# A linear-attention and two-stage expert kernel: two products moved from GpSimd to VectorE, a scan one unit later, one block's transposes sooner

## The chip, the core and the metric

One core of one Trainium2 chip runs the whole program. The metric is the device time of one execution in microseconds (us), the median of several runs. PE is TensorE, PEld its weight loads, DVE is VectorE, ACT is ScalarE, POOL is GpSimd, SP is the queue of SyncE, which issues nearly all loads.

## What is computed

Three layers follow each other. The first is a recurrent attention over 768 steps for 4 batches and 8 heads of width 48; its output is 3072 tokens of 384 numbers. The second is a gated layer without experts, and the third routes each token to two of eight experts.

```python
for t in range(S):                               # attention, per batch and head
    cur = np.einsum('bhd,bhe->bhde', u[None] * kt, vt)
    y[:, :, t] = np.einsum('bhd,bhde->bhe', rt, state + cur)
    state = wt[:, :, :, None] * state + np.einsum('bhd,bhe->bhde', kt, vt)
...
h = (x @ w1) * (x @ w2) @ w3                     # second layer
x = h @ w_out
...
out[mask] += top2_w[mask, k, None] * (np.maximum(x[mask] @ w1[e], 0.0) @ w2[e])
```

## The kernel before, in words

The tokens are cut into 24 chunks of 128 (six chunks for each batch) and 12 groups of two chunks. For the second layer the kernel first multiplies w3 by w_out, so that afterwards one matrix with 384 columns, and 16 columns for the routing of the third layer beside them, takes the place of two. This first stage is the one that the change touches. Each matrix is held as a high and a low part, so a product takes three matmuls (mm3, lines 193 to 196: high by high on line 194, high by low on 195, low by high on 196).

The work of the first stage comes in units u. A unit takes block u of w_out (128 x 384, cv_wo, only for u below 8) and block u of w3 (128 x 512, cv_w3). For each block ACT converts the top bits (line 149, tile top), DVE joins them with the middle bits (line 160 in the units written out by hand, line 178 later, tile cvz), ACT or DVE rounds this to the high part (167 or 180; WBh for w_out, w3h for w3), and DVE subtracts to get the low part (171 or 185; WBl, w3l). The joined w_out block is also transposed on PE (wo_T, line 420), copied out of PSUM (copy_T, lines 427 and 429, tile woT), multiplied by the routing weights (gate_cols, line 434), and the resulting 16 columns are split into high and low parts (gate_split, lines 139 and 140). mm_w3(u) then multiplies the w3 block by the finished w_out block. Units 0 to 2 are written out by hand in first_units (lines 444 to 492), where PE, DVE and ACT keep the order of the program. The loop of lines 619 to 637 runs units 3 to 18: at its start it converts, and the conversion calls flush, which joins and subtracts what the call before left open.

DVE keeps the order of the program throughout. The other engines are ordered by a planner until they are also put into program order (PE from group 2, ACT in the last group).

Between the units lie the attention's steps. WHEN (lines 548 to 553) gives, for each of the first six chunks, the slot of each of fourteen steps, in the order of STEPS (line 391). A slot of u - 24 up to u - 23.5 runs in the first half of unit u, ahead of mm_w3 and gate_split; the half unit after that runs behind wo_T. The steps that matter here, with their place in a line of WHEN counted from 0:

- 5, pre_scan (line 220): one DVE instruction that runs the product of the decays along the chunk (tile fg). It needs the load dtc.
- 9, pre_rec(j, 0) (lines 234 and 235): Ln and Exp on ACT, which give the reciprocals of fg (tile rc).
- 6, pre_rec(j, 1) (238 and 239): two DVE instructions that refine them. 7, pre_k, and 8, pre_r (do_r): two DVE instructions each, which scale k and r. do_r also issues the load dtc of chunk j + 2.
- 10, do_u: pre_u (lines 255 and 256), two products of 128 x 384 on the tile rku: r by k, and that by u. It also issues load_rk(j + 2), the load of r and k (tile nrk, two buffers) on SP.
- 11, pre_c (line 262): DVE sums the products of each head to cc. 12, pre_d (line 268): ACT spreads them over the diagonals of the tile am. 3, do_ov (line 280): DVE copies the masked attention products into am.
- 2, at_A (275), 4, do_T (285 and 287), 0, do_kv (308, then 315, 316 and 320) and 1, do_y (344, then 350 and 351): the attention's matmuls and what follows them. The last one leaves the tokens in high and low parts (xh, xl).

Behind the first stage the groups run: mo_ab (w1 and w2), mo_x (the merged matrix), then the routing; behind them the experts.

Of the kernel before, what the change touches and what calls it, by code (L numbers as in the profile page):

```python
# [71 lines left out]
def tile_kernel(ctx: ExitStack, tc: tile.TileContext, dt, nat, w3t, wout, w1, w2, e1, e2, cf, ci, out):  # L72
    nc = tc.nc
    pe, act, dve, pool, sp = nc.tensor, nc.scalar, nc.vector, nc.gpsimd, nc.sync
# [6 lines left out]
    class Pinned:  # L81
        on = False
# [7 lines left out]
    def f(ap):  # L90
        return ap.bitcast(F32)
# [14 lines left out]
    def c(n):  # L106
        o, w = CF[n]
        return cft[:, o:o + w]
# [29 lines left out]
    def split(h, l, src, on=None):  # L138
        act.copy(out=h, in_=src)
        (on or dve).tensor_tensor(out=l, in0=src, in1=f(h), op=OP.subtract)  # L140
# [18 lines left out]
    def join(mid, t, z, h, l, post):  # L159
        dve.scalar_tensor_tensor(z, mid, 13, t, op0=OP.logical_shift_right, op1=OP.bitwise_or)  # L160
        x = z.bitcast(F32)
        if post:
            post(x)
        return h, l, x

    def high(h, l, x, on=None):
        (on or act.copy)(out=h, in_=x)
        return h, l, x

    def lower(h, l, x):  # L170
        dve.tensor_tensor(out=l, in0=x, in1=f(h), op=OP.subtract)
# [21 lines left out]
    def mm3(o, wh, wl, xh, xl, start, stop, pin=lambda x: x):  # L193
        pin(pe.matmul(o, wh, xh, start=start, stop=False))  # L194
        pe.matmul(o, wh, xl, start=False, stop=False)  # L195
        pe.matmul(o, wl, xh, start=False, stop=stop)  # L196
# [54 lines left out]

    def pre_u(j):
        t = att.tile([P, DM], F32, name="rku", bufs=1)
        on = dve if 2 <= j < 5 else pool
        on.tensor_tensor(out=t, in0=RK[j][:, :DM], in1=RK[j][:, DM:], op=OP.mult)  # L255
        on.tensor_tensor(out=t, in0=t, in1=c("u"), op=OP.mult)
        KS["u", j] = t
# [106 lines left out]
    def do_u(j):  # L364
        pre_u(j)
        if j + 2 < NCH:
            load_rk(j + 2)
# [46 lines left out]
    def cv_wo(j, queue=True):  # L414
        return cvt(rawx["o", j], DM, woh[:, j, :DM], wol[:, j, :DM], post=lambda x: xo_.__setitem__(j, x), queue=queue)

    def wo_T(j, then=None):
        bank = PB[4 + j % 2]
        for kb in range(3):
            pe.transpose(bank[:, P * kb:P * kb + P], xo_[j][:, kb * P:kb * P + P], ident)  # L420
        (then or (lambda: copy_T(j)))()

    def copy_T(j):
        bank = PB[4 + j % 2]
        xo_[j] = fold.tile([P, DM], F32, name="woT")
        if j < 6:
            dve.tensor_copy(out=xo_[j], in_=bank[:, :DM])
        else:
            act.copy(out=xo_[j], in_=bank[:, :DM])

    def gate_cols(j):
        g = bK[:, 256 + 32 * j:272 + 32 * j]
        for kb in range(3):
            pe.matmul(g, xo_[j][:, P * kb:P * kb + P], wgn[:, kb], start=kb == 0, stop=kb == 2)  # L434

    def gate_split(j):
        split(woh[:, j, DM:], wol[:, j, DM:], bK[:, 256 + 32 * j:272 + 32 * j])

    def cv_w3(u, o=0, n=512, queue=True):
        if not o:  # L440
            w3s[u] = [fold.tile([P, 512], F32R, name=x, bufs=3) for x in ("w3h", "w3l")]
        return cvt(rawx["3", u], n, *[t[:, o:o + n] for t in w3s[u]], o, queue=queue)

    def first_units():
        x = cv_wo(0, False)
        o = high(*join(*x), dve.tensor_copy)
        wo_T(0, lambda: None)
        x = cv_w3(0, 0, 256, False)
        a = high(*join(*x))
        copy_T(0)  # L450
        warm_up(1)
        gate_cols(0)
        lower(*o)
        lower(*a)
        gate_split(0)
        mm_w3(0, (0, 1))
        x = cv_wo(1, False)
        o = join(*x)
        wo_T(1, lambda: None)
        x = cv_w3(0, 256, 256, False)  # L460
        b = join(*x)
        high(*o)
        high(*b)
        copy_T(1)
        lower(*b)
        mm_w3(0, (2,))
        gate_cols(1)
        x = cv_w3(1, 0, 256, False)
        a = high(*join(*x))
        lower(*o)  # L470
        gate_split(1)
        mm_w3(0, (3,))
        lower(*a)
        mm_w3(1, (0, 1))
        x = cv_w3(1, 256, 256, False)
        b = join(*x)
        x = cv_wo(2, False)
        high(*b)
        o = join(*x)
        lower(*b)  # L480
        mm_w3(1, (2,))
        wo_T(2, lambda: None)
        copy_T(2)
        mm_w3(1, (3,))
        x = cv_w3(2, queue=False)
        a = join(*x)
        high(*o)
        high(*a)
        gate_cols(2)
        lower(*o)  # L490
        gate_split(2)
        lower(*a)

    def mm_w3(u, fbs=range(4)):
        jb = u % 8
        for fb in fbs:
            s = slice(fb * P, fb * P + P)
            mm3(PB[fb][:, :XW], w3s[u][0][:, s], w3s[u][1][:, s], woh[:, jb, :], wol[:, jb, :], jb == 0, jb == 7,
                tc.keep_in_program_order if u == 15 else lambda x: x)
            if u == 7:  # L500
                split(W0[0][:, fb], W0[1][:, fb], PB[fb][:, :XW])
# [38 lines left out]
    def at(slot, fn, *a):  # L540
        todo.setdefault(slot, []).append((fn, a))

    def run_todo(lo, hi):
        for slot in sorted(x for x in todo if lo <= x < hi):
            for fn, a in todo.pop(slot):
                fn(*a)

    WHEN = {0: (-12.5, -11.5, -13.5, -12.5, -15.0, -20.6, -18.0, -17.05, -17.0, -20.0, -19.0, -16.5, -12.6, 0),
# [26 lines left out]
    for i, fn in enumerate(STEPS):  # L575
        for j in range(NCH):
            late = 3 if j == NCH - 1 and i == 1 else 0
            at(WHEN[j][i] if j in WHEN else 6 * j - 14 + LATE[i] - late, fn, j)
    at(-3, flush)
# [21 lines left out]
    def warm_up(n):  # L601
        for _ in range(n):
            tc.keep_in_program_order(pe.matmul(PB[6], warm, warm[:, None, :].to_broadcast([P, 4, P]), start=True, stop=True))
# [12 lines left out]
    with tc.manual_schedule(engines={mybir.EngineType.DVE, mybir.EngineType.PE, mybir.EngineType.Activation}):  # L616
        first_units()
# [718 lines left out]
```

## Time and profile before

| | before |
|---|---|
| median of 3 runs | 887.4 us (887.29 to 888.32) |
| profiled execution, its own time | 885.38 us |
| span of the profiled execution, first to last instruction | 883.6 us |
| PE busy | 867.0 us (98%) |
| DVE busy | 498.1 us (56%) |
| ACT busy | 435.9 us (49%) |
| POOL busy | 242.6 us (27%) |

The page gives each engine's busy time over the whole span. A busy share of 56% says nothing of one stage, so the trace is also read by stretches, and where two engines are both nearly always busy it is read instruction by instruction: the start, the duration, and in brackets the idle time of the engine just before, with what ended it. The chain of work that ended last follows the end of the program back, at each step to what released it.

### The profile page before, as it was taken

What the parts mean: (1) busy time and instruction counts of PE and PEld (TensorE: products, weight loads), DVE (VectorE), ACT (ScalarE), POOL (GpSimd) and SP (SyncE); (2) the same over time, 40 slices, a digit from 0 to 9 for tenths busy, and PEclk for the clock granted to TensorE, in tenths of its full rate; (3) what the DMA queues carried; (4) which work ended last, traced back from release to release, by engine and by line L of the source; (5) the groups of instructions that cost most, each with busy time, mean ns of one, the idle gap of its engine ahead of it and who ended that gap; (6) DMA issues with size and microseconds to landing.
All of it is one profiled execution on the core that took longest, in us unless ns stands there. A gap on an engine that the chain in (4) does not pass through costs nothing.

```text
span 883.6 us, 18266 instructions
## 1 busy us (share of the span) xinstructions
PE 867.0 (98%) x7325; PEld 807.5 (91%) x7325; DVE 498.1 (56%) x1219; ACT 435.9 (49%) x880; POOL 242.6 (27%) x216
## 2 busy tenths in 40 slices
PE   8999999999999999999999999999999999999996
PEld 5789899999999999999999989899998998989896
DVE  6899874866756856765475453352534434343430
ACT  5777665566466456555454343433433344343431
POOL 2010021041141141232344443407052260603113
PEclk9999999999999999999999999999999999999999
DMA  9956399668476566443365798829467393854213
GB/s 344 387 212 210 93 129 238 163 142 220 119 200 162 156 180 127 96 122 108 83 164 121 187 246 210 211 56 240 85 182 185 94 212 67 245 118 102 27 14 47
DMA packets 124255, 139.22 MB, mean 158 GB/s; under 512 B 75008, under 2 KB 103680, under 8 KB 124160
## 3 DMA queue, kind: packets, MB, share of 16 engines
q1 hardware_dynamic: 100624, 109.58, 45.9%
q0 software_dynamic: 12160, 19.72, 11.8%
q10 hardware_dynamic: 11376, 8.65, 3.1%
q8 instruction: 59, 0.97, 0.5%
q14 instruction: 36, 0.29, 0.1%
HBM read 88.12 MB, written 36.04 MB: 141 GB/s over the span
## 4 chain that ended last, share of the span: by engine, by line
PE 89%; DVE 6%; ACT 2%; issue 1%; DMA 0%; POOL 0%; SPq 0%; POOLq 0%; DVEq 0%; ACTq 0%
PE pb L194 27%; PE pb L195 26%; PE pb L196 26%; PE pb L344 3%; PE pb L275 3%; PE pb L1014 1%; DVE cvz L178 1%; PE pb L308 1%; DVE fg L222 0%; DVE w3l L185 0%; DVE am L280 0%; DVE WAl L185 0%; DMA rawf<-w3t 0%; PE pb L434 0%; ACT top L149 0%
## 5 line engine op out<-in xcount | busy, mean ns | idle before, releaser
L1019 POOL DMA_INDIRECT out<-ye,ti x49 | 77.0, 1572 | 225.7 <-ACT ye L1009 205.3
L992 DVE SCALAR_TENSOR_TENSOR HH<-pb,HH 128x256 fp32r<-128x256 f32 (+1 forms) x128 | 71.2, 557 | 110.6 <-ACT HH L991 110.6
L194 PE MATMUL pb<-XTh,WAh 128*128 128x512 f32 (+1 forms) x384 | 131.7, 343 | 0.0
L196 PE MATMUL pb<-XTh,WAl 128*128 128x512 f32 (+1 forms) x384 | 131.4, 342 | 0.0
L195 PE MATMUL pb<-XTl,WAh 128*128 128x512 f32 (+1 forms) x384 | 131.0, 341 | 0.0
L194 PE MATMUL pb<-WBh,HH 128*128 128x384 f32 x384 | 129.3, 337 | 0.0
L196 PE MATMUL pb<-WBh,HH 128*128 128x384 f32 x384 | 128.4, 334 | 0.0
L195 PE MATMUL pb<-WBl,HH 128*128 128x384 f32 x384 | 128.3, 334 | 0.0
L991 ACT ACTIVATE HH<-pb 128x256 fp32r<-128x256 f32 (+1 forms) x128 | 62.8, 492 | 115.4 <-PE pb L196 113.3
L824 POOL DMA_INDIRECT slots<-g_sc,g_si x48 | 51.7, 1077 | 125.2 <-DVE g_si L823 69.5
L1009 ACT ACTIVATE ye<-pb,ti 128x384 f32<-128x384 f32 x42 | 24.4, 582 | 124.2 <-PE pb L196 124.2
L195 PE MATMUL pb<-xl,WAh 128*128 128x256 f32 x288 | 80.8, 281 | 0.8 <-DVE xl L351 0.8
L194 PE MATMUL pb<-xh,WAh 128*128 128x256 f32 x288 | 81.5, 283 | 0.0
L194 PE MATMUL pb<-xh,WBh 128*128 128x256 f32 x288 | 81.2, 282 | 0.0
L195 PE MATMUL pb<-xl,WBh 128*128 128x256 f32 x288 | 81.0, 281 | 0.0
L196 PE MATMUL pb<-xh,WBl 128*128 128x256 f32 x288 | 81.0, 281 | 0.0
L196 PE MATMUL pb<-xh,WAl 128*128 128x256 f32 x288 | 80.9, 281 | 0.0
L195 PEld LDWEIGHTS pb<-XTl,WAh 128*128 128x128 f32 x384 | 72.3, 188 | 7.6
L196 PEld LDWEIGHTS pb<-XTh,WAl 128*128 128x128 f32 x384 | 72.2, 188 | 7.6
L194 PEld LDWEIGHTS pb<-XTh,WAh 128*128 128x128 f32 x384 | 72.0, 188 | 7.5
L194 PEld LDWEIGHTS pb<-WBh,HH 128*128 128x128 f32 x384 | 72.1, 188 | 5.0 <-ACT WAh L892 4.4
L255 POOL TENSOR_TENSOR rku<-nrk 128x384 f32<-128x384 f32 x21 | 21.7, 1031 | 197.7 <-DVE cc L262 80.8
(208 smaller groups left out, 2065.7 us busy)
## 6 DMA issues: line engine op xcount, KB each, us to landing
dtc<-dt SPq DMA_DIRECT2D x24, 772.0 KB, 5.2
raw<-e SPq DMA_DIRECT2D x18, 768.0 KB, 5.5
raww<-e SPq DMA_DIRECT2D x14, 768.0 KB, 5.2
nrk<-nat SPq DMA_DIRECT2D x24, 384.0 KB, 6.8
expert_rows<-xg SPq DMA_DIRECT2D x45, 192.0 KB, 6.1
rawf<-w3t SPq DMA_DIRECT2D x14, 512.0 KB, 7.2
nv<-nat SPq DMA_DIRECT2D x24, 256.0 KB, 5.4
out<-zeros SPq DMA_DIRECT2D x9, 576.0 KB, 5.4
```

Source lines behind the costliest of these rows:

```text
L178: dve.scalar_tensor_tensor(z, mid, 13, t, op0=OP.logical_shift_right, op1=OP.bitwise_or)
L194: pin(pe.matmul(o, wh, xh, start=start, stop=False))
L195: pe.matmul(o, wh, xl, start=False, stop=False)
L196: pe.matmul(o, wl, xh, start=False, stop=stop)
L255: on.tensor_tensor(out=t, in0=RK[j][:, :DM], in1=RK[j][:, DM:], op=OP.mult)
L275: pe.matmul(bST[hb][:, P * a:P * a + P], KT[j][q, a].rearrange("p s i -> p (s i)"), RT[j][q, a].rearrange("p s i -> p (s i)"), start=True, ...
L344: pe.matmul(o, lt, rh, start=st, stop=en, tile_position=tp)
L824: ins = pool.indirect_dma_start(out=table, out_offset=bass.IndirectOffsetOnAxis(ap=si[:, i, k:k + 1], axis=0), in_=SC[:, i, k, :], in_offs ...
L991: act.activation(out=Hh[hf][:, ff], in_=bank[:, :n], func=AF.Relu)
L992: dve.scalar_tensor_tensor(Hl[hf][:, ff], bank[:, :n], 0.0, f(Hh[hf][:, ff]), op0=OP.max, op1=OP.subtract)
L1009: act.activation(out=y[:n], in_=bank[:n], func=AF.Copy, scale=wt)
L1019: ins = pool.indirect_dma_start(out=out, out_offset=bass.IndirectOffsetOnAxis(ap=ti(e, j)[:, 0:1], axis=0), in_=y[:n], in_offset=None, com ...
```

## The change

Chunks 0 and 1 get their two products of r, k and u on VectorE, as chunks 2 to 4 have them already; from chunk 5 on they stay on GpSimd. For chunk 0 the products move from unit 5 to unit 7, right behind the scaling of r and just ahead of pre_c; for chunk 1 from the second half of unit 9 to the second half of unit 11, between the scaling of k and of r. The scan of chunk 0 moves from unit 3 to unit 4, the Ln and Exp of its reciprocals from unit 4 to unit 5. In first_units the transposes of w_out's third block (block 2) stand ahead of two quarters of mm_w3(1) instead of between them, and the copy that follows stands ahead of both quarters.

```diff
     def pre_u(j):
         t = att.tile([P, DM], F32, name="rku", bufs=1)
-        on = dve if 2 <= j < 5 else pool
+        on = dve if j < 5 else pool
         on.tensor_tensor(out=t, in0=RK[j][:, :DM], in1=RK[j][:, DM:], op=OP.mult)
         on.tensor_tensor(out=t, in0=t, in1=c("u"), op=OP.mult)
...
         high(*b)
         o = join(*x)
+        wo_T(2, lambda: None)
         lower(*b)
-        mm_w3(1, (2,))
-        wo_T(2, lambda: None)
         copy_T(2)
-        mm_w3(1, (3,))
+        mm_w3(1, (2, 3))
         x = cv_w3(2, queue=False)
...
-    WHEN = {0: (-12.5, -11.5, -13.5, -12.5, -15.0, -20.6, -18.0, -17.05, -17.0, -20.0, -19.0, -16.5, -12.6, 0),
-            1: (-8.5, -6.0, -8.9, -8.5, -9.5, -14.5, -12.3, -12.1, -12.0, -13.5, -14.5, -12.0, -10.3, 0),
+    WHEN = {0: (-12.5, -11.5, -13.5, -12.5, -15.0, -19.6, -18.0, -17.05, -17.0, -19.0, -16.55, -16.5, -12.6, 0),
+            1: (-8.5, -6.0, -8.9, -8.5, -9.5, -14.5, -12.3, -12.1, -12.0, -13.5, -12.05, -12.0, -10.3, 0),
```

## Rows read from the trace of the kernel before

**Rows 1.** Profile page, busy time and share of the span.

```profile
PE 867.0 (98%) x7325; PEld 807.5 (91%) x7325; DVE 498.1 (56%) x1219; ACT 435.9 (49%) x880; POOL 242.6 (27%) x216
```

**Rows 2.** Stretches: busy us of PE, PEld, DVE, ACT, POOL; clock, DMA share, GB/s.

```profile
20.00:25.00 5.00, 3.10 (x21) 2.66 (x21) 4.86 (x8) 2.68 (x8) 2.62 (x2) 1.00 1.03 407
...
130.00:200.00 70.00, 70.00 (x859) 67.87 (x860) 46.21 (x129) 42.07 (x91) 17.08 (x16) 1.00 0.80 180
```

**Rows 3.** Chain that ended last, to 130 us: start, us, what.

```profile
111.33 0.34 DVE rt L250
```

**Rows 4.** Timeline of POOL: start us, us, line, operation [idle before <-releaser].

```profile
19.98 1.43 POOL L255 TENSOR_TENSOR rku<-nrk 128x384 f32<-128x384 f32 x1 [0.70 <-DMA nrk<-nat]
21.49 1.21 POOL L256 TENSOR_TENSOR rku<-rku,cft 128x384 f32<-128x384 f32 x1
44.59 1.02 POOL L255 TENSOR_TENSOR rku<-nrk 128x384 f32<-128x384 f32 x1 [21.90 <-DMA nrk<-nat]
```

**Rows 5.** Timeline of DVE beside these POOL instructions, units 4 and 11.

```profile
19.40 0.68 DVE L178 SCALAR_TENSOR_TENSOR cvz<-rawf,top 128x512 int32<-128x512 int32 x1
...
20.47 1.35 DVE L178 SCALAR_TENSOR_TENSOR cvz<-rawf,top 128x384 int32<-128x384 int32 x1
21.75 1.50 DVE L185 TENSOR_TENSOR w3l<-cvz,w3h 128x512 fp32r<-128x512 f32 x1
23.17 0.17 DVE L140 TENSOR_TENSOR WBl<-pb,WBh 128x16 fp32r<-128x16 f32 x1
...
44.63 1.54 DVE L178 SCALAR_TENSOR_TENSOR cvz<-rawf,top 128x512 int32<-128x512 int32 x1 [0.70 <-ACT top L149]
46.09 1.50 DVE L185 TENSOR_TENSOR w3l<-cvz,w3h 128x512 fp32r<-128x512 f32 x1
```

**Rows 6.** Timeline of PE in the first stage.

```profile
14.20 0.49 PE L420 MATMUL pb<-cft,cvz 128*128 128x128 f32 x3
...
21.88 0.55 PE L420 MATMUL pb<-cft,cvz 128*128 128x128 f32 x3 [1.50 <-DVE cvz L178]
...
47.65 0.45 PE L196 MATMUL pb<-WBh,w3l 128*128 128x400 f32 x1 [0.79 <-DVE w3l L185]
...
52.47 1.00 PE L196 MATMUL pb<-WBh,w3l 128*128 128x400 f32 x4
```

**Rows 7.** Timeline of DVE, first stage: third block's join and copy, scan, two waits.

```profile
12.51 1.01 DVE L160 SCALAR_TENSOR_TENSOR cvz<-rawf,top 128x256 int32<-128x256 int32 x2
...
14.73 0.56 DVE L427 COPY woT<-pb 128x384 f32<-128x384 f32 x1 [0.87 <-PE pb L420]
...
17.80 1.24 DVE L222 TENSOR_TENSOR_SCAN fg<-dtc,d 128x520 f32<-128x520 f32 x1
...
37.65 0.17 DVE L140 TENSOR_TENSOR WBl<-pb,WBh 128x16 fp32r<-128x16 f32 x1 [0.38 <-ACT WBh L139]
...
38.75 0.69 DVE L185 TENSOR_TENSOR w3l<-cvz,w3h 128x512 fp32r<-128x512 f32 x1 [0.33 <-ACT w3h L180]
```

**Rows 8.** DVE groups by shape to 112 us: busy us, mean ns, idle before.

```profile
L178 DVE SCALAR_TENSOR_TENSOR cvz<-raw,top 128x384 int32<-128x384 int32 x12 | 6.4, 549 | 0.0
```

**Rows 9.** Timeline of ACT, idle before a gate split, and the last am columns.

```profile
24.80 0.17 ACT L139 CAST WBh<-pb 128x16 fp32r<-128x16 f32 x1 [1.74 <-PE pb L434]
...
46.73 0.69 ACT L268 ACTIVATE am<-cft,cc 128x128 f32<-128x128 f32 x2
```

**Rows 10.** Timeline of DVE, products as chunk 4 has them, first and what follows.

```profile
107.73 0.55 DVE L255 TENSOR_TENSOR rku<-nrk 128x384 f32<-128x384 f32 x1
...
108.79 0.68 DVE L238 TENSOR_TENSOR kt<-fg,rc 128x512 f32<-128x512 f32 x1
```

**Rows 11.** DMA issue at 36.10 us: queue, count, KB each, us to landing.

```profile
nrk<-nat SPq DMA_DIRECT2D x1, 384.0 KB, 8.3
```

**Rows 12.** Timeline of DVE behind the products' new place in unit 11.

```profile
51.74 0.68 DVE L185 TENSOR_TENSOR w3l<-cvz,w3h 128x512 fp32r<-128x512 f32 x1
...
60.52 0.36 DVE L315 TENSOR_TENSOR stmp<-pb,snew 128x192 f32<-128x192 f32 x1 [1.31 <-PE pb L308]
```

## The prediction, made before the changed kernel was run

> **What bounds the kernel now.** I read the page first: PE is busy for 98% of the span [rows 1], so at most some 16 us can be won anywhere, and only where PE is idle. The second view, busy time by stretches, says where: from 130 us on PE is busy all the time [rows 2], while between 20 and 25 us it works 3.10 of 5 us and DVE 4.86 [rows 2]. The change touches nothing behind 55 us, so whatever it wins or loses must be won or lost in the first stage and must then be carried to 130 us. The third view, the chain that ended last, tells how it is carried: from 60 to 111 us the chain lies mostly on DVE, and its last DVE link is the scaling of r at 111.33 [rows 3]; from there PE has it. So an advance at 60 us reaches the end if DVE has it too, not PE alone. The last view is the timeline of each engine between 12 and 62 us. There are two places where POOL makes its two products, for chunk 0 from 19.98 to 22.70 and for chunk 1 from 44.59 to about 47.0 [rows 4] (the fourth instruction repeats the second). Beside each of them two DVE instructions are long: 1.35 and 1.50 us in unit 4, 1.54 and 1.50 in unit 11 [rows 5]. The same shapes take 0.549 us as a mean of twelve elsewhere for 128x384 [rows 8], and 0.68 for 128x512 [rows 5, 12]. PE waits for just these: 1.50 us at 21.88, 0.79 us at 47.65 [rows 6].
>
> **What POOL's products cost DVE.** The excess is 0.80 + 0.82 = 1.62 us in unit 4 and 0.86 + 0.82 = 1.68 us in unit 11. All four instructions read two SBUF tensors, and each begins while POOL works on a product; POOL's own first product is long as well, 1.43 against 1.02 [rows 4]. I take it that they hold each other up, and that the excess vanishes with POOL's instructions. The Trainium skill (SBUF — State Buffer, section "SBUF: two separate sides") says the same: a DVE instruction with two SBUF inputs and a GpSimd instruction that reads SBUF lock each other out for a whole instruction. By the rule the 1.35 us one would have waited until POOL's end at 21.41 and finished at 21.96; the row has 21.82, so the trace agrees within 0.14.
>
> **What the products cost on DVE.** Chunk 4 has them there: from the first product's start to the next independent instruction it is 108.79 - 107.73 = 1.06 us [rows 10]. So each chunk pays 1.06 and gets back 1.62 or 1.68. What that is worth depends on the places.
>
> **Unit 2, the third block's transposes.** DVE has joined the block at 13.52 (12.51 + 1.01), but PE transposes it only at 14.20, behind a quarter of mm_w3(1), and DVE sits idle 0.87 us before the copy at 14.73 [rows 6, 7]. In the new order they can start at about 13.58, so copy, the next join and all that hangs on them come 14.20 - 13.58 = 0.62 sooner. The matmuls that are put behind them fill the time in which PE waited for the copy; they cost nothing. Bounds: 0 and the 0.87 of idle time. Gain 0.6.
>
> **Units 3 and 4, the scan.** It leaves its place ahead of the copy of block 3's transpose, which had to wait for it a little (I take 0.2; between 0 and the 1.24 of the scan [rows 7]), and comes behind the second long instruction, ahead of the gate split that is now at 23.17 [rows 5]. There it costs what it took before, 1.15 until the next instruction could start. So at the gate split DVE is at 23.17 - 0.62 - 0.2 - 1.62 + 1.15 = 21.88, which is 1.3 sooner. PE's waits around it close by as much. ACT's next conversions hang on the following transposes and columns, and ACT sat idle for 1.74 us there, until 24.80 [rows 9], so all of unit 5 comes 1.3 sooner. The Ln and Exp of chunk 0, now in unit 5, fit into that hole: about 1.2 us, and needed only by the refining two units later. If the planner puts them ahead of a conversion instead, they cost up to 1.2 (a rival below). The scan's load landed long before.
>
> **Unit 7, chunk 0's products.** They stand behind the scaling of r, so at_A is not held; behind them in DVE's queue are gate split 6, pre_c and the next joins, which come 1.06 later: DVE is only 0.25 ahead. But DVE then waits twice for ACT, 0.38 at 37.65 and 0.33 at 38.75 [rows 7], and ACT is 1.3 ahead, so 0.7 to 0.9 comes back: DVE is about 1.0 ahead. PE needs these results later than that and keeps its 1.3. On SP the load of r and k for chunk 2 moves from 27.5 to about 34.8, and chunk 1's, which reuses the buffer that the product reads, comes right behind it. Before, chunk 1's was issued at 36.10 and took 8.3 us [rows 11]; with 384 KB more ahead of it, one more us at the 407 GB/s of the loaded queue [rows 2], it lands at about 44.4 again. POOL waited for it; now DVE would, at about 49. That leaves 4.5 us of cover; beyond it each us late would be a us lost. Loads issued behind it (w3's last blocks, chunk 1's v) are used at 53 us or later. POOL has nothing queued behind what it loses until 112 us.
>
> **Unit 11, chunk 1's products.** Without POOL the two long instructions end 1.68 sooner, so DVE would be 2.7 ahead, and PE, whose 0.79 of waiting goes, 2.1 to 2.3. What is late next is ACT's last pair of am columns, 46.73 to 47.42 [rows 9], which DVE's masked copy needs; ACT is some 1.3 to 2 ahead (it also waited a little for the long join). So DVE goes on 1.9 to 2.1 ahead, does the refining and the scaling of k, then pays 1.06 for the products, and comes to the low part of block 10 (51.74 [rows 12]) about 1.0 ahead. PE used that low part at 52.47, 0.05 us behind its end [rows 6, 12]. So PE stands here, at 51.4, and its advance drops from over 2 to 1.1. From there PE has no idle time to speak of until 60, where DVE waits 1.31 us for PE [rows 12]: both are then 1.1 ahead, and the DVE chain of rows 3 carries that to 111 us. load_rk(3) now waits for the later product, but with the loads of w1 and w2 ahead of it in the queue; nothing needs it before 90 us.
>
> **The sum.** Span 883.6 - 1.1 = 882.5, the profiled execution's own time 885.38 - 1.1 = 884.3. The median of the runs, 887.4, lies 2.0 above the profiled execution; carried over, that gives 887.4 - 1.1 = **886.3 us**, 0.12% faster. A measurement of this kernel can tell about 0.2%, or 1.8 us, from no change, so this counts as no change.
>
> **Rivals.**
>
> *PE isn't held at block 10.* If the planner puts other work of PE there, or ACT brings the am columns sooner so that DVE arrives 2 ahead, PE's whole advance of 2.1 to 2.7 reaches 60 us, and DVE's idle 1.31 there lets DVE follow. For it: the wait rests on two rows that lie 0.05 apart, and DVE has slack. Against it: DVE's order is fixed and the products stand ahead of that instruction. Time 887.4 - 2.3 = 885.1; with the bounds of unit 2 and of the scan down to 884.4. It counts as faster.
>
> *The reciprocals get in the way.* The planner puts Ln and Exp ahead of unit 5's conversions: 1.2 of the 1.3 is gone, later pieces give back 0.2 to 0.4. Time 887.1. The idle 1.74 speaks against it.
>
> *DVE is too full for them (slower).* If the four long instructions are long for another reason, say the loads that run at full rate just then, they stay long, and DVE gets 2 x 1.06 on top. Unit 4 then gives -0.62 - 0.2 + 1.15 = +0.33, unit 7 +1.06 less 0.8 of idle, and unit 11 +1.06, which is 1.6 at block 10: 889.0; where the idle time hides nothing, 2.4, or 889.8. It decides at the two long joins: if they stay over 1.3 us with POOL silent, this is the case. Against it: the join at 19.40, under the same loads, takes 0.68 for a larger block [rows 5], and only the four beside POOL are long. The Trainium skill (Perfetto Trace Analysis, section "Optimizing Scalar/DVE Operations") says that with a saturated DVE, handing work to GpSimd may make sense, which is the reverse of this change, but adds that between these two it might not help since they share a port; the long rows bear out the second half.
>
> **How the numbers follow.** Forecast 0.52 (886.3; own range 885.6 to 887.0), PE not held 0.28 (885.1), reciprocals 0.10 (887.1), DVE too full 0.10 (889.0). The range leaves out the lower end of the second case and the upper half of the last one: 884.6 to 888.4. Faster by over 0.2% means below 885.6: nearly all of the second case and a little of the first, 0.31. Slower by over 0.2% means above 889.2: about half of the last case and something unforeseen in the planner's order, 0.07. The rest is 0.62.
>
> **What would show it.** Right, step by step: no DVE join or subtraction over 0.7 us between 20 and 48 us; the copy of block 2's transposes near 14.1; gate split 3 near 21.9; the products at about 34.3 and 49.3, 0.55 each, without a wait for nrk; PE's waits of 1.50 and 0.79 gone and a new one of about 1 us for the low part of block 10, near 50 to 51; the masked sum at 59.4 instead of 60.52; the last scaling of r in the chain near 110.2. The forecast is wrong if the advance at 60 us isn't the one that is left at 111 us, if PE's or ACT's order in units 5 to 12 differs much, or if the products wait for their load.

## The result, and the profile after

The changed kernel takes 893.4 us as a median of ten executions, the kernel before 887.95 beside it (884.95 to 890.74): ratio 1.0065, interval 1.0045 to 1.0085. One of the ten took 1068.3 us at a mean granted clock of 0.749 and is left out of the ratio; the other nine take 891.4 to 896.9, with a median of 892.8. A second set of executions gave 1.0049 [1.0029, 1.0069]. By the means of the two sets it is slower by 5.8 and 4.1 us; the forecast was 886.3, with 888.4 as its upper end.

The changed kernel was profiled in both sets: spans of 893.6 and 889.3 us. I call them the first and the second profile of the changed kernel. First what went as forecast. DVE in the first profile (start us, us, engine, line, operation, x count [idle before <-releaser]):

```profile
25.68 0.69 DVE L185 TENSOR_TENSOR w3l<-cvz,w3h 128x512 fp32r<-128x512 f32 x1
26.28 1.23 DVE L222 TENSOR_TENSOR_SCAN fg<-dtc,d 128x520 f32<-128x520 f32 x1
27.43 0.15 DVE L140 TENSOR_TENSOR WBl<-pb,WBh 128x16 fp32r<-128x16 f32 x1
...
41.89 0.55 DVE L255 TENSOR_TENSOR rku<-nrk 128x384 f32<-128x384 f32 x1
42.48 0.56 DVE L256 TENSOR_TENSOR rku<-rku,cft 128x384 f32<-128x384 f32 x1
...
67.77 0.36 DVE L315 TENSOR_TENSOR stmp<-pb,snew 128x192 f32<-128x192 f32 x1 [2.45 <-PE pb L308]
...
118.51 0.42 DVE L250 TENSOR_TENSOR rt<-dtc,fg 128x256 f32<-128x256 f32 x1
```

No join or subtraction is long any more (0.69 where [rows 5] have 1.50), the products take 0.55 and 0.56 and wait for no load, and the scan costs 27.43 - 26.28 = 1.15. But the masked sum of block 1, `stmp`, stands at 67.77 instead of 60.52 [rows 12] and follows a wait of 2.45 instead of 1.31. From there nothing is lost or won for a long time: `stmp` to the scaling of r is 50.74 us here and 50.73 before, where that is this instruction, whose chain piece is [rows 3]:

```profile
111.25 0.42 DVE L250 TENSOR_TENSOR rt<-dtc,fg 128x256 f32<-128x256 f32 x1
```

In all sixteen profiles, fourteen of them of the experiments below, it is 332.9 us from `stmp` to PE's last but one group of L275 (393.39 us in the kernel before). What is left of the span behind `stmp` is 823.1 to 826.3 us, with the kernel before at both 823.1 and 824.7, and this spread has two parts. From `stmp` to the start of the program's last write to `out` it is 816.7 to 818.8 us, with the kernel before at both 816.7 and 818.3; that doesn't go with the change. From the start of that write to the end of the span it does: 6.2 to 6.4 us in the five profiles with the products on POOL, 7.4 to 8.0 in the eleven with the products on DVE. The last write, and behind it what the queue of instructions moved (kind: packets, MB, share of 16 engines); first the kernel before, with a span of 883.6, then the second profile of the changed kernel:

```profile
877.18 1.56 POOL L1019 DMA_INDIRECT out<-ye,ti  x1 [2.60 <-ACT ye L1009]
q14 instruction: 4, 0.03, 1.5%
...
881.34 1.56 POOL L1018 DMA_INDIRECT out<-ye,ti  x1 [2.60 <-ACT ye L1008]
q14 instruction: 5, 0.04, 1.8%
```

That is 6.42 us against 7.96. The packets are five in all eleven and four in all five; whether the fifth is the reason no run shows. So the change costs some 1.5 us at the very end of the program, and the rest ahead of `stmp`, in the first 68 us.

Two views show where in these 68 us. The granted clock by stretches (columns as in [rows 2]; the clock stands third from the end), first profile:

```profile
5.00:10.00 5.00, 3.71 (x19) 2.79 (x18) 3.46 (x9) 2.40 (x7) 0.00 (x0) 0.92 0.97 352
10.00:15.00 5.00, 4.68 (x18) 4.14 (x17) 2.81 (x8) 2.50 (x8) 0.00 (x0) 0.50 1.02 419
15.00:20.00 5.00, 5.00 (x21) 4.86 (x19) 2.25 (x5) 2.34 (x5) 0.31 (x1) 0.55 1.04 405
20.00:25.00 5.00, 3.96 (x24) 3.47 (x24) 2.87 (x6) 2.45 (x6) 0.00 (x0) 1.00 0.97 330
25.00:30.00 5.00, 3.59 (x17) 3.01 (x15) 3.91 (x7) 2.63 (x5) 0.00 (x0) 0.63 0.71 190
30.00:35.00 5.00, 4.90 (x23) 4.43 (x22) 2.60 (x6) 2.43 (x5) 0.00 (x0) 0.69 0.60 226
```

And PE's waits of over 0.7 us between 5 and 64 us of the same profile:

```profile
7.33 0.84 PE L434 MATMUL pb<-cft,woT 128*128 128x16 f32 x6 [1.02 <-DVE woT L427]
...
24.68 1.00 PE L194 MATMUL pb<-WBh,w3h 128*128 128x400 f32 x4 [0.78 <-ACT w3h L180]
27.63 0.70 PE L195 MATMUL pb<-WBl,w3h 128*128 128x400 f32 x1 [1.27 <-DVE WBl L140]
38.60 0.81 PE L434 MATMUL pb<-cft,woT 128*128 128x16 f32 x6 [0.92 <-ACT top L149]
...
58.81 1.01 PE L196 MATMUL pb<-WBh,w3l 128*128 128x400 f32 x4 [1.63 <-DVE w3l L185]
61.61 0.63 PE L196 MATMUL pb<-WBh,w3l 128*128 128x400 f32 x2 [1.06 <-DVE w3l L185]
```

PE's 1.50 and 0.79 of [rows 6] are gone. In their place stand 0.78 and 1.27 in unit 4, and 1.63 and 1.06 at blocks 10 and 11 (the 0.92 at 38.60 is there before as well, at 32.28). And twice PE's clock is at 0.50, the lower of its two levels (1.2 GHz), where in the profile that the prediction rests on it is 1.00 all the way to 60 us.

So beside the end of the program there are three suspects: the order of unit 4, the place of chunk 1's products, and the clock.

### The profile page after: what moved, and what is told of

Same layout as the page of the kernel before. It is cut to its first block, busy times and chain, and to the rows that moved or that the text cites. A ratio compares the mean times of both kernels' runs of the same rounds, so it can differ in the third digit from the quotient of the medians.

```text
span 893.6 us, 18266 instructions
## 1 busy us (share of the span) xinstructions
PE 872.6 (98%) x7325; PEld 814.1 (91%) x7325; DVE 496.6 (56%) x1223; ACT 435.2 (49%) x880; POOL 235.9 (26%) x212
## 4 chain that ended last, share of the span: by engine, by line
PE 89%; DVE 6%; ACT 2%; issue 1%; DMA 0%; POOL 0%; SPq 0%; POOLq 0%; ACTq 0%; DVEq 0%
PE pb L194 27%; PE pb L196 26%; PE pb L195 26%; PE pb L344 3%; PE pb L275 3%; PE pb L1013 1%; PE pb L308 1%; DVE cvz L178 1%; PE pb L434 1%; DVE am L280 1%; ACT top L149 1%; DMA rawf<-w3t 0%; DVE WAl L185 0%; DVE fg L222 0%; DVE w3l L185 0%
## 5 line engine op out<-in xcount | busy, mean ns | idle before, releaser
L255 POOL TENSOR_TENSOR rku<-nrk 128x384 f32<-128x384 f32 x19 | 19.2, 1009 | 209.4 <-DVE cc L262 130.0
```

## The experiments

The following ran in four sets, each on another chip, with the kernel before beside them: medians 888.55, 888.12, 887.79 and 887.45 us. "Half" is the time at half clock per execution, 2 x (1 - mean granted clock) x span, as a mean over the executions. It counts the end of the program too: in the sixteen profiles the clock is at 0.50 for the last 2.3 to 6.4 us, behind the last matmul. To compare places I use two stretches that show little of what the clock did earlier: **A** from the first high matmul of w3's block 2 (16.66 us in the kernel before) to unit 6's gate columns (32.28), and **B** from there to `stmp` (60.52). Before: A 15.62, B 28.24.

| kernel | us | ratio [interval] | half, us | A | B |
|---|---|---|---|---|---|
| before, again | 888.66 | 1.0006 [0.9985, 1.0027] | 11.8 | fell | 27.19 |
| transposes alone | 887.66 | 1.0000 [0.9980, 1.0019] | 9.8 | 14.89 | fell |
| products alone | 889.12 | 1.0004 [0.9984, 1.0025] | 9.3 | 14.42 | fell |
| scan alone | 889.70 | 1.0013 [0.9995, 1.0030] | 10.9 | fell | 27.39 |
| changed, again | 892.43 | 1.0049 [1.0029, 1.0069] | 13.7 | 16.17 | 29.22 |
| without the transposes | 893.01 | 1.0049 [1.0032, 1.0065] | 14.3 | fell | 29.20 |
| scan back | 890.41 | 1.0030 [1.0014, 1.0047] | 12.7 | 14.40 | 29.20 |
| scan back, later products | 887.44 | 0.9991 [0.9973, 1.0009] | 11.4 | 14.36 | 26.87 |
| changed, ACT's order kept | 888.60 | 1.0017 [1.0001, 1.0033] | 9.9 | 14.96 | fell |
| the same, later products | 886.55 | 0.9987 [0.9967, 1.0007] | 10.2 | 14.95 | 26.85 |
| before, dummy matmuls | 887.13 | 1.0001 [0.9983, 1.0018] | 9.2 | fell | 27.49 |
| scan back, later, dummies | 883.90 | 0.9959 [0.9943, 0.9976] | 6.0 | 14.29 | 26.85 |
| changed, dummies | 889.66 | 1.0020 [1.0004, 1.0036] | 9.3 | fell | 29.20 |
| ACT's order, later, dummies | 885.62 | 0.9983 [0.9965, 1.0001] | 6.8 | 15.04 | 26.86 |

"Fell" means that the clock fell inside that stretch of that profile. The changed kernel's first profile has B at 29.17.

**The kernel before again** (no edit), to see how its executions differ, and **the three parts alone**. The first is the third block's transposes ahead of the quarter of w3's block 1:

> The kernel before once more, unchanged, for the granted clock of each of its executions. Theory A (the changed order makes PE idle at new places in units 3 to 5, and the clock falls for that): the mean granted clock stays at 0.997 or more in nearly all executions, times 885 to 890 us. Rival B (the fall of the clock at 9 us is luck: it comes ahead of every changed instruction, so the kernel before must suffer it as often): several executions at 0.994 or below, and those are the slow ones, by 2 to 5 us.

```diff
-        lower(*b)
-        mm_w3(1, (2,))
         wo_T(2, lambda: None)
+        lower(*b)
         copy_T(2)
-        mm_w3(1, (3,))
+        mm_w3(1, (2, 3))
```

> Kernel before with the third block's transposes alone moved ahead. Theory A: PE idles less near 15 us, clock 0.997 or more, time 886.8 to 888.3, no difference from before. Rival C (the moved transposes are what sets the clock off): clock 0.994 or below, 890 us or more.

The second is the products on DVE with their new places, the scan where it was:

```diff
-        on = dve if 2 <= j < 5 else pool
+        on = dve if j < 5 else pool
...
-    WHEN = {0: (-12.5, -11.5, -13.5, -12.5, -15.0, -20.6, -18.0, -17.05, -17.0, -20.0, -19.0, -16.5, -12.6, 0),
-            1: (-8.5, -6.0, -8.9, -8.5, -9.5, -14.5, -12.3, -12.1, -12.0, -13.5, -14.5, -12.0, -10.3, 0),
+    WHEN = {0: (-12.5, -11.5, -13.5, -12.5, -15.0, -20.6, -18.0, -17.05, -17.0, -20.0, -16.55, -16.5, -12.6, 0),
+            1: (-8.5, -6.0, -8.9, -8.5, -9.5, -14.5, -12.3, -12.1, -12.0, -13.5, -12.05, -12.0, -10.3, 0),
```

> Kernel before with the products of chunks 0 and 1 alone moved to DVE, in their new slots; scan, reciprocals and transposes as before. Theory A: the long joins are gone, clock 0.997 or more, time 886 to 888. Rival D (DVE is too full for the products): 889 us or more at a full clock, with DVE late at the low part of block 10.

The third is the scan and its reciprocals a unit later, products on POOL:

```diff
-    WHEN = {0: (-12.5, -11.5, -13.5, -12.5, -15.0, -20.6, -18.0, -17.05, -17.0, -20.0, -19.0, -16.5, -12.6, 0),
+    WHEN = {0: (-12.5, -11.5, -13.5, -12.5, -15.0, -19.6, -18.0, -17.05, -17.0, -19.0, -19.0, -16.5, -12.6, 0),
```

> Kernel before with chunk 0's scan and reciprocals alone one unit later (products stay on POOL in their old slots). ACT's order changes with it: the gate split of block 3, which waits for PE, comes ahead of the conversion of w_out's block 4. Theory A: PE has over 1 us of idle time near 24 us, the clock is 0.994 or below in most executions, time 890 us or more. Rivals B, C and D: no change from before, 886 to 889 us.

Measured: 1.0000, 1.0004 and 1.0013, all within the interval's reach of no change. No part alone costs what the whole costs. The products alone (889.1 us) miss the 886 to 888 that was expected; their profile has the late end, 7.6 us behind the last write. In seven of the twelve executions of the kernel before the mean clock is 0.994 or less, and these are the seven slowest (888.5 to 893.0 us against 886.5 to 888.2): the clock falls in the kernel before too, as the rival B had it.

The profile of the kernel before again has a span of 887.0 us, 3.4 more than the profile that I predicted from. Its clock fell behind PE's wait in unit 4, which is 2.30 us there and not the 1.50 of [rows 6]; PE, and the stretch behind it:

```profile
22.50 0.55 PE L420 MATMUL pb<-cft,cvz 128*128 128x128 f32 x3 [2.30 <-DVE cvz L178]
```

```profile
25.00:30.00 5.00, 5.00 (x19) 4.86 (x20) 1.25 (x3) 2.43 (x5) 0.00 (x0) 0.51 0.71 267
```

It was 35.10 - 32.28 = 2.82 us late at unit 6's gate columns, but only 1.77 at `stmp` (62.29): it got back 1.05. A reason is seen in unit 11. The long joins there depend on how POOL's products fall against DVE's, and in this execution the second is hardly held (POOL, then DVE, same profile; before in [rows 4, 5] 1.54 and 1.50):

```profile
45.88 1.03 POOL L255 TENSOR_TENSOR rku<-nrk 128x384 f32<-128x384 f32 x1 [23.86 <-DVE W0l L140]
46.99 1.02 POOL L256 TENSOR_TENSOR rku<-rku,cft 128x384 f32<-128x384 f32 x1
```

```profile
47.45 1.10 DVE L178 SCALAR_TENSOR_TENSOR cvz<-rawf,top 128x512 int32<-128x512 int32 x1 [0.69 <-ACT top L149]
48.48 0.68 DVE L185 TENSOR_TENSOR w3l<-cvz,w3h 128x512 fp32r<-128x512 f32 x1
```

So the excess that the change removes in unit 11 was 0.42 us in this execution and 1.68 in the one that I costed. With the products on POOL, B is 27.2 to 27.5 in the three profiles where unit 6's gate columns come at 34.7 us or later, and 28.24 in the one where they come at 32.28: lateness is partly made good there. If a gain is partly lost in the same way, that would explain why the transposes alone bring nothing; no run isolates it.

**The whole and the whole less one part.** The changed kernel again; it without the transposes; it with the scan in its old place:

> The changed kernel once more, unchanged, on a chip on which the kernel before is timed with its clock beside it. Theory E (two things add up: PE's new waits of 2.7 us for the low parts of blocks 10 and 11, against 0.8 to 1 us before, are worth 1 to 2 us at an equal clock; the rest is more time at the low clock in units 0 to 6, because PE idles more there): about 891 to 893 us, some 3 to 4 us above before, with 3 to 6 us more at the low clock than before on average. Rival F (the chip or the hour of the first comparison did it): within 1 us of before.

```diff
+        lower(*b)
+        mm_w3(1, (2,))
         wo_T(2, lambda: None)
-        lower(*b)
         copy_T(2)
-        mm_w3(1, (2, 3))
+        mm_w3(1, (3,))
```

> The changed kernel with the third block's transposes put back behind a quarter of mm_w3(1); products and the later scan stay. Theory E: as the two parts alone added up to, 1.3 us for the products and 0.5 for the scan, so 1.5 to 2.5 us above before. Rival C (the transposes make the clock fall in company with the others): less than 1 us above before.

```diff
-    WHEN = {0: (-12.5, -11.5, -13.5, -12.5, -15.0, -19.6, -18.0, -17.05, -17.0, -19.0, -16.55, -16.5, -12.6, 0),
+    WHEN = {0: (-12.5, -11.5, -13.5, -12.5, -15.0, -20.6, -18.0, -17.05, -17.0, -20.0, -16.55, -16.5, -12.6, 0),
```

> The changed kernel with chunk 0's scan and reciprocals back in their old slots; products on DVE and transposes ahead stay. Theory E: the products' 1 to 1.5 us stays, PE still waits 2.7 us for blocks 10 and 11; ACT's order in unit 4 is that of before, so the clock is as before; 0.5 to 1.5 us above before. Rival G (the scan is the main cause): no difference from before.

The loss repeats (1.0049). It doesn't hang on the transposes: without them it is 4.9 us, above the 1.5 to 2.5 that was expected. With the scan back it is 2.3 us (1.0030), above the expected 0.5 to 1.5 too, and smaller than with the scan moved, though the intervals overlap. Stretch A is 14.40 with the scan back and 16.17 with it moved. What the scan does to A is seen on ACT, in the second profile of the changed kernel:

```profile
19.49 0.51 ACT L180 CAST WBh<-cvz 128x384 fp32r<-128x384 f32 x1 [0.61 <-DVE cvz L178]
21.81 0.17 ACT L139 CAST WBh<-pb 128x16 fp32r<-128x16 f32 x1 [1.81 <-PE pb L434]
21.88 0.62 ACT L180 CAST w3h<-cvz 128x512 fp32r<-128x512 f32 x1
22.40 0.64 ACT L149 ACTIVATE top<-rawf 128x384 f16<-128x384 bf16 x1
...
25.41 0.63 ACT L234 ACTIVATE rc<-fg 128x512 f32<-128x512 f32 x1 [0.55 <-DVE fg L222]
```

The kernel before has them so:

```profile
19.61 0.62 ACT L149 ACTIVATE top<-rawf 128x384 f16<-128x384 bf16 x1
...
20.61 0.60 ACT L180 CAST w3h<-cvz 128x512 fp32r<-128x512 f32 x1
21.12 0.17 ACT L139 CAST WBh<-pb 128x16 fp32r<-128x16 f32 x1
```

There the top of wout's block 4 and the cast of w3's block 3 come first, and the gate split L139 of unit 3 then finds PE done. In the changed kernel the split stands ahead of both and waits 1.81 us for PE. The split comes first in all five profiles with the scan moved and ACT left to the planner, and in none of the eight with the scan in its old place, so it is the scan's move that brings it to the front. PE waits for the cast (0.78), DVE for the top (1.13), and then PE again for DVE's part of the split, which stands behind the scan (1.27).

**Chunk 1's products one step later**, behind the scaling of r (`pre_r`) of the same chunk, on top of the scan back:

```diff
-            1: (-8.5, -6.0, -8.9, -8.5, -9.5, -14.5, -12.3, -12.1, -12.0, -13.5, -12.05, -12.0, -10.3, 0),
+            1: (-8.5, -6.0, -8.9, -8.5, -9.5, -14.5, -12.3, -12.1, -12.0, -13.5, -12.0, -12.0, -10.3, 0),
```

> As the run with the scan put back, but chunk 1's products one step later, behind the scaling of r, so that the low part of block 10 doesn't wait for them; the planner then puts PE's at_A(1) and transposes ahead of the low part of block 11 again. Theory E: PE's waits for blocks 10 and 11 fall from 2.7 to under 1 us, the masked sum of chunk 1 comes 1 to 2 us sooner, time 1 to 2 us below the run with the scan put back, so 0 to 1 us below before. Rival D (DVE is simply too full): no gain against that run, since DVE does the same work.

B falls from 29.20 to 26.87 us, the time from 890.4 to 887.4. PE in the second profile of the changed kernel, then in this one:

```profile
54.62 1.00 PE L196 MATMUL pb<-WBh,w3l 128*128 128x400 f32 x4 [1.62 <-DVE w3l L185]
...
57.42 0.64 PE L196 MATMUL pb<-WBh,w3l 128*128 128x400 f32 x2 [1.06 <-DVE w3l L185]
...
59.00 0.60 PE L285 MATMUL pb<-cft,kt 128*128 128x128 f32 x4
59.53 1.16 PE L275 MATMUL pb<-rt,kt 48*128 48x128 f32 x16
```

```profile
52.58 0.99 PE L196 MATMUL pb<-WBh,w3l 128*128 128x400 f32 x4 [0.56 <-DVE w3l L185]
...
54.96 1.16 PE L275 MATMUL pb<-rt,kt 48*128 48x128 f32 x16
56.05 0.66 PE L285 MATMUL pb<-cft,kt 128*128 128x128 f32 x4
56.56 1.00 PE L196 MATMUL pb<-WBh,w3l 128*128 128x400 f32 x4
```

The wait at block 10 is 1.06 shorter, the length of the two products. The second wait has gone altogether: with r scaled in time, PE again does the chunk's own matmuls (L275, L285) ahead of block 11's low part, as in the kernel before. In the changed kernel they stand behind it, so PE is idle for 1.06 us with work at hand, and `stmp`, which waits for PE behind those matmuls, is late.

**ACT's order of unit 4 kept**, by recording ACT's instructions of `cv_wo(4)` and of gate split 3 where they stand, on the changed kernel; and the same with the later products:

```diff
+            act.on = u == 4
...
+            act.on = False
```

> The changed kernel, but in unit 4 ACT's instructions are recorded by hand in the order that the kernel before has there: the conversions of block 4's transposes and of w3's block ahead of gate split 3. Theory: the move of the scan costs time only because the planner then puts gate split 3, which waits for PE, ahead of those conversions. Then the 1.8 us that the kernel with the scan left in its old place has over the changed kernel come back: the masked sum of block 1 starts some 1.8 us sooner after the first matmul of w3's block 2 (about 43.6 instead of 45.4 us), and the time is 1.5 to 2 us under the changed kernel's 892.4, as far as the clock is alike. Rival (it is the scan's own 1.15 us on DVE, in a place where DVE has no slack): DVE's order is the same, so the stretch stays at 45.0 to 45.6 us and the time within 0.7 us of 892.4.

> As the run with ACT's order of unit 4 by hand, and chunk 1's products put behind the pair that follows them, as in the run with later products. Theory (two separate causes, ACT's order in unit 4 and the place of chunk 1's products, and nothing else): both are cured, the stretch from the first matmul of w3's block 2 to the masked sum of block 1 is 41.0 to 41.6 us as in the run with later products (41.23), and the time is 886.5 to 888, 0.999 of the kernel before. Rival (the scan costs by itself): the stretch is 42.5 to 43.2 us and the time some 889 us.

With the order kept, A is 14.96 and 14.95 instead of 16.17. ACT and PE of the first of the two:

```profile
23.30 0.62 ACT L86 CAST w3h<-cvz 128x512 fp32r<-128x512 f32 x1 [0.98 <-DVE cvz L178]
24.24 0.51 ACT L180 CAST WBh<-cvz 128x384 fp32r<-128x384 f32 x1 [0.32 <-DVE cvz L178]
24.66 0.17 ACT L86 CAST WBh<-pb 128x16 fp32r<-128x16 f32 x1
```

```profile
24.26 0.55 PE L420 MATMUL pb<-cft,cvz 128*128 128x128 f32 x3 [0.69 <-DVE cvz L178]
24.88 1.00 PE L194 MATMUL pb<-WBh,w3h 128*128 128x400 f32 x4
26.08 0.46 PE L195 MATMUL pb<-WBl,w3h 128*128 128x400 f32 x1 [0.20 <-DVE WBl L140]
```

PE's wait of 1.27 is 0.20. (The split stands one cast later than in the kernel before, behind that of w_out's block 4; DVE gets to its own part of the split only at 25.88, behind the scan, so that costs nothing.) So of the 1.77 that the scan's move cost in A, 1.21 were ACT's order, and some 0.56 go with the scan's new place on DVE. The ratio fell from 1.0049 to 1.0017, or 2.8 us, more than the 1.5 to 2 us expected, but the times don't confirm the 1.21: beside the first the kernel before has 8.6 us at half clock, beside the second 12.8, so the changed kernel went from 5.0 us more than it to 2.9 less, and by the line given below (0.32 us per us) that alone is 2.5 us. The reading rests on stretch A. With both causes cured the sum of A and B is 41.80; I expected 41.0 to 41.6 without a price of the scan and 42.5 to 43.2 with its full one, so it pays part.

**Dummy matmuls in PE's wait ahead of unit 0's gate columns**, six groups instead of one, on four kernels. What they compute is used nowhere.

```diff
-        warm_up(1)
+        warm_up(6)
```

> The kernel before, but with six groups of the dummy matmuls instead of one ahead of the first gate columns, so that PE has work in its wait at 6 to 7 us. Theory (the spread between executions and a part of the changed kernel's loss come from TensorE's granted clock, which falls to half in the first stage after waits of PE, and costs 0.38 us for each us at half): the fall that begins near 9 us is rarer, the time at half clock goes from about 9 to 4 to 6 us on average, and the time is 1 to 2 us under the kernel before. Rival (the clock falls whatever PE does in that wait, or the time at half clock is only where PE waits anyway): mean clock and time as before, within 0.7 us, or 0.5 us more for the dummy matmuls.

> The kernel with the scan in its old place and the later products of chunk 1, with the six groups of dummy matmuls as well. Theory of the clock: 4 to 6 us less at half clock than the run without them (11.4 on average), and a time 1.5 to 2.3 us under its 887.4: some 885.5. Rival: no difference in clock or time, 887 to 888.

> The changed kernel with six groups of dummy matmuls instead of one in PE's wait ahead of the first gate columns. Theory (two parts: some 1.7 us of the loss are half clock, some 2.5 us are the order of the work): the time at half clock goes from 13.7 us on average to 6 to 9, the time from 892.4 to 889 to 890.5, so 1.5 to 3 us above the kernel before stay. Rival 1 (the clock is all of it): 887 to 888.5, no difference from the kernel before. Rival 2 (the clock is a consequence and costs nothing): 891.5 to 893.

> The changed kernel with ACT's order of unit 4 by hand, chunk 1's products one step later, and six groups of dummy matmuls. The same without the dummy matmuls took 886.55 us, and the kernel with the scan in its old place, later products and dummy matmuls 883.9. Theory (the scan's new place costs some 0.6 us of the first stage once ACT's order is cured, the rest is clock): 884.2 to 885.2 us, with some 6 us at half clock. Rival (the scan's new place is free or a gain): 883.0 to 884.0. The masked sum of block 1 tells it apart: 41.7 to 41.9 us behind the first matmul of w3's block 2 by the theory, 41.0 to 41.2 by the rival.

In the sixteen profiles the wait ahead of those columns is from nothing to 2.09 us. In the six profiles where it was 0.46 or less, all four with the dummies among them, the clock stayed at 1.00 until 20 us; in the ten where it was 0.76 or more it fell to 0.50 before 10 us. The fall is missing in four of four profiles with the dummies and in two of twelve without, so they take the first fall away. Whether a second one comes in units 4 and 5 goes with PE's waits there. The changed kernel with dummies, PE and stretch, and then the scan back with later products and dummies:

```profile
23.30 0.70 PE L195 MATMUL pb<-WBl,w3h 128*128 128x400 f32 x1 [1.27 <-DVE WBl L140]
```

```profile
25.00:30.00 5.00, 4.91 (x20) 4.43 (x20) 1.97 (x5) 2.43 (x5) 0.00 (x0) 0.63 0.78 281
```

```profile
21.35 0.55 PE L420 MATMUL pb<-cft,cvz 128*128 128x128 f32 x3 [0.79 <-DVE cvz L178]
```

```profile
25.00:30.00 5.00, 4.61 (x28) 3.54 (x26) 4.45 (x9) 3.36 (x7) 0.00 (x0) 1.00 1.03 411
```

The kernel before with dummies gained nothing (887.1, I expected 1 to 2 us less): its first fall is gone, but its profile has the 2.30 us wait of unit 4, and the clock fell there instead. The changed kernel with dummies took 889.66, inside the 889 to 890.5 of the theory of two parts; neither "all clock" (887 to 888.5) nor "clock costs nothing" (891.5 to 893) fits, even if they are set lower by the 0.7 us that the kernel before is faster in this set. Against the kernel before with dummies it is 889.7 - 887.5 = 2.2 us slower as a mean, at the same time at half clock (9.3 and 9.2 us). That is the price of all but the clock: the order in the first stage and the end of the program, where these two profiles differ by 1.4 us. The scan back with later products and dummies has neither fall: **883.9 us, 0.9959 [0.9943, 0.9976]**, faster than both kernels and than the 885.5 expected. With the scan moved and ACT's order kept it is 885.62, a little over the 884.2 to 885.2 expected; A + B is 41.90, as the theory had it (41.7 to 41.9), and 41.14 without the move, so the scan's new place still costs 0.8 us of the first stage. The two times differ by 1.7 us, with intervals that overlap; where more than 0.8 would come from isn't shown.

## Why the prediction was wrong

The forecast's sum is -0.62 (unit 2), -0.67 (units 3 and 4: -0.2 - 1.62 + 1.15) and +0.2 (an advance of 1.3 that drops to 1.1 by block 10), with nothing behind 55 us. Three of its steps failed: ACT's order in unit 4, PE's order behind block 10, and the end of the program. At full clock the profiles give, part by part:

- **Unit 2: right.** From the first high matmul of unit 0 (8.88 and 8.86 us) to that of block 2 (17.43 and 16.84) it is 8.55 us in the kernel before and 7.98 with the new order, both with dummies and at full clock: -0.57.
- **What POOL's products cost DVE: right.** The long instructions are gone with POOL's. The rival that DVE is too full for them falls. The Trainium skill (SBUF — State Buffer, section "SBUF: two separate sides") has them exclude each other for a whole instruction. The execution where POOL and DVE met differently fits that: the join begun at 47.45 would wait for POOL's end at 48.01 and finish at 48.69, and the row has 48.55. But I took the excess of one execution as a constant.
- **Units 3 and 4: the first failed step.** That DVE is at the gate split at 21.88 was worked out for DVE alone, with ACT as it stood. I looked at where the planner would put Ln and Exp (they did fit the hole, at 25.41) and not at where it would put the gate split. With the planner's order A is 16.17 - 15.62 = +0.55 instead of -0.67: error 1.2 us. With ACT's order kept it is 14.96 - 15.62 = -0.66, just the forecast, but partly by luck: with the scan in its old place A falls by 1.2 (14.40), not by the 1.62 of the excess, and the scan's move costs 0.56, not 1.15 - 0.2 = 0.95.
- **Unit 7: right.** Chunk 0's products delayed nothing that counted: with the scan back, PE reaches block 10's low part 53.43 - 33.19 = 20.24 us after unit 6's gate columns, 20.19 before.
- **Unit 11: half right.** PE is held at block 10's low part, as forecast, by the length of the products. What I said follows, "from there PE has no idle time to speak of", is the second failed step: PE's own order changed, and the wait of 1.06 at block 11 came on top. B is 29.22 - 28.24 = +0.98 instead of +0.2, and nearly all of it lies behind block 10's low part (54.62 to 63.62 is 9.00 us, 52.47 to 60.52 was 8.05). Taking the products behind `pre_r` shows it: 26.87, which is 1.4 better than before.
- **From 60 us on: right to 393 us, and the third failed step at the end.** What was lost at `stmp` was carried unchanged that far. But "the change touches nothing behind 55 us" left out that it takes four instructions from POOL, whose last write ends the program: the stretch behind it grew from 6.4 to 7.9 us, by 1.5, and by 1.2 with the products alone. That it comes with the products is shown by the sixteen profiles; how, is open.

So the sum at full clock is -0.57 + 0.55 + 0.98 + 1.5 = +2.5 us, not -1.1. Measured are 5.8 and 4.1. The forecast's frame was wrong as well: it held one profiled execution for typical, at full clock in the whole first stage, and carried the difference over to the median. Over 125 executions of the kernel before the time ranges from 882.8 to 892.1 us and the time at half clock goes with it (correlation 0.78; a line through them rises 0.32 us per us at half clock, lines through single sets 0.35 to 0.42). The changed kernel has 13.7 to 14.7 us at half clock, the kernel before 8.6 to 12.9 in the four sets. By that line the changed kernel's second set lost (13.7 - 8.6) x 0.32 = 1.6 us to the clock. Part of that seems the change's own doing: in seven of the sixteen profiles PE has waits of over 0.6 us in units 3 to 5 that add up to 1.87 us or more, in five by ACT's order and in two, of the kernel before, by POOL's products at their worst, and in six of these seven the clock fell between 20 and 32 us; in the other nine it didn't fall there. It isn't a rule for all falls: two profiles have one near 33 us, behind the wait of 0.92 that every profile has, and one has it near 55.5, behind a wait of 1.63 at block 10, where six others waited 1.62 to 1.65 without one.

For the second set, 4.1 us slower as a mean, that makes 2.5 + 1.6 = 4.1 us. That it fits so closely is luck. The time at half clock counts the end of the program as well, where PE is done, and the slope is 0.32 to 0.42; and the kernel before makes good some 1 us of lateness in B (27.2 to 27.5 where it is late) while the changed one has 29.2 whenever it gets there, which the line may hold in part. The scan back with later products is a second test: -0.57, 41.23 - 43.86 = -2.63 for A and B, and 1.2 at the end are -2.0 at full clock; 2.7 us more at half clock add 0.9, which makes -1.1, and its mean is 0.8 below the kernel before. Why the first set shows 5.8 isn't settled: the clock of the kernel before isn't on record there.

The rival "PE isn't held at block 10" falls: PE is held, by more than forecast. "The reciprocals get in the way" had the right engine, ACT, and the wrong instruction: its 887.1 supposed that Ln and Exp would stand ahead of the conversions, and the gate split did.

## What to carry to other kernels

When a planner orders the instructions of each engine, a moved step has to be followed into every engine's queue: ask which waits now stand ahead of work that was ready, since an engine that takes its instructions in order turns one early wait into waits on two others. Put work that two engines don't need yet behind the step that feeds the next matmuls, not ahead of it. Look at the end of the program too when an engine that works there loses instructions: here 1.2 to 1.5 us were lost some 800 us behind the change. And before costing a change of a few microseconds, look at how the executions of the kernel before differ: here much of the spread came from PE's clock and from how two engines happened to collide, and both were in the stretch that was being changed.

## What the runs showed of the hardware

PE's clock fell to half in the first stage in all ten profiles with a wait of 0.76 to 2.09 us ahead of unit 0's gate columns, and in none of the six where that wait was 0.46 us or less did it fall before 20 us. Around the wait of 1.02 in the first profile PE was at work for 3.71 of 5 us. I had expected falls only of long idle times.

One us at half clock went with 0.32 us of time over all sets, and with 0.35 to 0.42 within one. The Trainium skill (TensorE: Matmul & The Clock Gate, section "Terms") puts the penalty at the throttled time times the missing share of the clock, which would be 0.5. The runs are under that; 2.3 to 6.4 us of the time at half clock lie behind the last matmul, and some of the rest may lie where PE waits for other engines anyway, which no run isolates.

Dummy matmuls in the right wait (1.61 us for the six groups) are worth it only if the next wait doesn't bring the same fall: nothing in the kernel before, some 3 us in the one whose later waits are short (887.4 to 883.9, or 0.9991 to 0.9959 of the kernel before beside it, with 11.4 and 6.0 us at half clock).

With the products on DVE the end of the span came 7.4 to 8.0 us behind the start of POOL's last write, in eleven of eleven profiles, and 6.2 to 6.4 with them on POOL, in five of five; the queue of instructions moved five packets there instead of four.
